# New planning constants for a fused attention and GEGLU kernel

## The chip, the cores and the metric

The kernel runs on one core of one Trainium2 chip. The metric is the device time of one execution in microseconds; the core has a matrix engine (TensorE, PE), a vector engine (VectorE, DVE), a scalar engine (ScalarE, ACT), GpSimd (POOL) and a sync engine (SyncE, SP) that issues the DMAs. Each engine runs its own instructions strictly in the order of the program and waits on semaphores for the others.

## The reference

One transformer block on 2048 rows of width 640: attention with 32 heads of 20 columns behind a LayerNorm, then a gated MLP of width 1728 behind a second LayerNorm, each with its residual.

```python
def _A_ref(x, wqkv, wo):
    B, S, D = x.shape
    H = 32
    Dh = D // H
    qkv = (x @ wqkv).reshape(B, S, 3, H, Dh) ...
    scores = jnp.einsum("bhqd,bhkd->bhqk", q, k) * (Dh ** -0.5)
    p = _softmax(scores, axis=-1)
    o = jnp.einsum("bhqk,bhkd->bhqd", p, v)
    return o ... @ wo

def _B_ref(x, w_gate, w_up, w_down):
    g = jnp.einsum("bsd,df->bsf", x, w_gate)
    u = jnp.einsum("bsd,df->bsf", x, w_up)
    h = _gelu(g) * u
    return jnp.einsum("bsf,fd->bsd", h, w_down)

h = x + _A_ref(_layernorm(x, axis=-1), A_wqkv, A_wo)
h2 = h + _B_ref(_layernorm(h, axis=-1), B_w_gate, B_w_up, B_w_down)
return h2
```

## The kernel before

**Tiles, slots and units.** The queries are worked in eight chunks (SIZES: 512, five of 256, two of 128 rows). The heads form eight groups of four. A *slot* is 512 columns of queries: one head group for the chunk of 512, two for 256, four for 128; there are 32 slots, 0 to 31. Each slot has 64 score tiles of 128 keys by 512 query columns, four of them (one for each head of the group) making a *quad*. The scores of a tile are one row-tiled product, since a head has only 20 columns and four heads sit in four strips of 32 rows (`qk_mms`, L1059). Tiles go through in *units* (`unit`, L1035): alternately three tiles in the PSUM banks 0 to 2 and two in the banks 3 and 4. ACT takes the exponential of a whole unit in one instruction, 1536 or 1024 columns wide (emitted through a helper, so the profile names L437), and writes it to a ring of 19 tiles (`pts`, and a part of `rege`).

**Tiles on DVE.** D_SLOT says how many quads of a slot do not go to ACT but to DVE. Such a tile's scores go to a spare bank (5 or 7), or, for as many of the slot's tiles as D_RING allows, to the third bank of a three-bank unit, which then has only two tiles for ACT. DVE first turns the scores into 16-bit integers (`d_exp`, L972) and, when a quad has its four tiles, makes four terms from them (2048 wide each, L437), whose sum as bf16 stands for the exponential. Each term is a value product of its own. SUMS says how many pairs of terms DVE adds beforehand, each of which saves one value product. D_SPAN spreads the tiles over the slot.

**Value products.** A quad's four tiles meet the values in column tiling: four strips of 32 columns, one for each head, in bank 6 (`pv_op`, L995). `unit` issues them when PV_QUADS quads are complete, two here. Values of a later slot wait until the last product of the slot before is in, and its `epilogue` (L1128) has copied bank 6 to `osb`. The epilogue then normalizes, for most slots through DRAM (`spread`, L1106), for the last ones of a chunk through PE transposes (L1159 to L1203).

**Around it.** Ahead of the first scores stand the first LayerNorm, the transposes of its result (L662), the key, query and value projections (L745, L887), and a bound on the scores (L772, L871, L875) that is subtracted through an extra row of the product. Later projections, and for each finished chunk the output projection (L740), second LayerNorm, transposes (L662 on PE for the chunks in XP_PE, a DMA for the others), gate and up products (L1314 and L740), GELU and down product (L1383 and L740) are filled in between the scores and value products of the next chunk (`post`, L1230). For the last chunk they stand at the end, behind the last exponential.

**What sets the order.** No order is written by hand. Every operation is recorded with an estimated duration and a priority, and a planner in the program (`Sched.schedule`, L100) makes each engine's order when the program is built. It keeps the constants below:

- QK_LEAD, by slot: how long before ACT is due PE is kept free for the next scores (L254).
- PE_AGE, by slot: how long an operation in another tiling may wait before PE changes its tiling for it (L177); the tilings are row, column and full.
- SD_AGE and SD_ROW, by slot: how long a DVE tile's scores wait for a row-tiled stretch (L165).
- P_..., the priorities (a lower number goes first); P_EV those of DVE operations that free a bank, P_KP those of the first key projection, P_RS those of the LayerNorm's statistics, P_ADD those of the residual sums.
- HOLD, K1_AFTER, V_HOLD, Q1_HOLD: evacuations or products of the front that are held back until the bound of the first head group is ready; V_ACT, XN_DVE and K1_ACT: which evacuations of the front go to ACT and which to DVE.
- PAD_MIN: where PE's recent use is low, value products get up to four idle matmuls with a zero operand as filler.

The check that decides how many quads are issued at once:

```python
if n < PV_QUADS and left:
    return
quads = [pv_wait[4 * k:4 * k + 4] for k in range(min(n, PV_QUADS if left or s_ < len(slots) - 1 else 1))]
```

## Time and profile before

| | |
|---|---|
| Median of 3 runs | 867.11 us (866.93 to 867.78) |
| The profiled execution | 867.46 us |
| Its span, first to last instruction | 865.7 us |
| Granted TensorE clock | 1.00 throughout |
| First exponential starts | 33.0 us |
| Exponentials of 1024 columns | 454 |
| Exponentials of 1536 columns | 264 |
| DVE tiles (L972) | 348 |

The span can be read in three parts. In the front the input comes in, is normalized and projected. The middle is the long run of exponentials. At the end the last chunk's MLP runs. A group's mean duration covers the whole of an instruction, while the next one of the same engine already begins, so the distance from start to start is shorter than the mean. The engines' shares are averages over all three parts; the prediction reads them by stretch.

### The profile page before, as it was taken

What the parts mean: (1) busy time and instruction counts of PE and PEld (TensorE: products, weight loads), DVE (VectorE), ACT (ScalarE), POOL (GpSimd) and SP (SyncE); (2) the same over time, 40 slices, a digit from 0 to 9 for tenths busy, and PEclk for the clock granted to TensorE, in tenths of its full rate; (3) what the DMA queues carried; (4) which work ended last, traced back from release to release, by engine and by line L of the source; (5) the groups of instructions that cost most, each with busy time, mean ns of one, the idle gap of its engine ahead of it and who ended that gap; (6) DMA issues with size and microseconds to landing.
All of it is one profiled execution on the core that took longest, in us unless ns stands there. A gap on an engine that the chain in (4) does not pass through costs nothing.

```text
span 865.7 us, 35516 instructions
## 1 busy us (share of the span) xinstructions
PE 835.9 (97%) x16187; PEld 420.8 (49%) x16219; DVE 748.5 (86%) x1371; ACT 839.4 (97%) x806; POOL 93.7 (11%) x268
## 2 busy tenths in 40 slices
PE   7999999999999899999999999999999999999998
PEld 5533332322344344445455555555554556666667
DVE  8859999999898899797899989999999897998344
ACT  7899999999999999999999999999999999999992
POOL 5001111110001210101002010011102110010000
DMA  7211122123102442001110201010101201020000
GB/s 274 84 50 57 32 71 61 46 71 93 53 4 67 128 146 80 16 18 36 53 42 16 36 8 61 5 35 17 49 19 24 58 8 31 19 48 11 2 18 17
DMA packets 47485, 42.54 MB, mean 49 GB/s; under 512 B 18628, under 2 KB 41952, under 8 KB 47336
## 3 DMA queue, kind: packets, MB, share of 16 engines
q1 hardware_dynamic: 47336, 40.27, 16.0%
q8 instruction: 127, 2.08, 1.0%
q14 instruction: 22, 0.18, 0.1%
HBM read 27.95 MB, written 10.26 MB: 44 GB/s over the span
## 4 chain that ended last, share of the span: by engine, by line
ACT 45%; PE 42%; DVE 11%; issue 1%; DVEq 0%
ACT pts L437 30%; ACT rege L437 14%; PE ps L1059 13%; PE ps L437 11%; PE ps L740 10%; PE ps L745 3%; DVE qt_all L437 2%; PE ps L887 2%; DVE rege L437 2%; DVE rege L972 2%; PE ps L1314 1%; DVE qt_all L972 1%; DVE stats L437 1%; ACT qt_all L437 1%; PE ps L1383 1%
## 5 line engine op out<-in xcount | busy, mean ns | idle before, releaser
L437 ACT ACTIVATE pts<-ps 128x1024 bf16<-128x1024 f32 (+1 forms) x496 | 558.3, 1232 | 2.9 <-PE ps L1059 2.1
L1059 PE MATMUL ps<-qt_all,kt_all 32*128 32x256 bf16 (+2 forms) x4096 | 307.1, 273 | 11.2 <-ACT pts L437 5.2
L437 ACT ACTIVATE rege<-ps 128x1024 bf16<-128x1024 f32 (+1 forms) x222 | 247.6, 1192 | 0.4 <-PE ps L1059 0.2
L1059 PEld LDWEIGHTS ps<-qt_all,kt_all 32*128 32x128 bf16 x4096 | 104.2, 92 | 198.1 <-ACT pts L437 83.0
L972 DVE TENSOR_SCALAR rege<-ps 128x512 int16<-128x512 f32 x220 | 148.2, 683 | 19.4 <-PE ps L1059 18.1
L437 PE MATMUL ps<-rege,v_all 128*21 128x256 bf16 (+2 forms) x2201 | 140.3, 286 | 1.3 <-DVE rege L437 0.5
L437 PE MATMUL ps<-pts,v_all 128*21 128x256 bf16 (+2 forms) x2403 | 124.7, 273 | 1.0 <-DVE osb L437 0.8
L740 PE MATMUL ps<-rege,regw 128*32 128x256 bf16 (+1 forms) x2600 | 120.5, 296 | 1.5 <-DVE rege L972 0.5
L972 DVE TENSOR_SCALAR qt_all<-ps 128x512 int16<-128x512 f32 x128 | 86.5, 682 | 11.9 <-PE ps L1059 11.4
L437 DVE TENSOR_SCALAR rege<-rege 128x2048 int16<-128x2048 int16 x141 | 94.5, 686 | 2.5 <-PE ps L437 1.9
L740 PEld LDWEIGHTS ps<-rege,regw 128*32 128x32 bf16 x2600 | 60.4, 96 | 34.6 <-issue 20.1
L437 PEld LDWEIGHTS ps<-rege,v_all 128*21 128x21 bf16 x2201 | 54.1, 91 | 42.7 <-issue 25.2
L437 PEld LDWEIGHTS ps<-pts,v_all 128*21 128x21 bf16 x2403 | 57.0, 91 | 26.1 <-issue 18.4
L740 PE MATMUL ps<-regw,rege 128*32 128x320 bf16 x1296 | 68.1, 301 | 0.7 <-issue 0.4
L437 DVE TENSOR_SCALAR qt_all<-qt_all 128x2048 int16<-128x2048 int16 (+4 forms) x113 | 65.4, 589 | 2.8 <-ACT qt_all L437 1.1
L437 PE MATMUL ps<-qt_all,v_all 128*21 128x256 bf16 (+1 forms) x1264 | 56.4, 264 | 0.8 <-DVE qt_all L437 0.8
L437 DVE TENSOR_SCALAR qt_all<-rege 128x2048 int16<-128x2048 int16 x80 | 53.8, 684 | 1.5 <-PE ps L437 0.9
L745 PE MATMUL ps<-regw 128*128 128x512 bf16 x176 | 52.5, 383 | 2.0 <-issue 1.1
L437 POOL TENSOR_SCALAR rn<-rc 128x16 int32<-128x16 int32 x22 | 6.7, 305 | 393.3 <-DMA rc<-sums 393.1
L1368 DVE TENSOR_TENSOR rege<-rege,ps 128x512 bf16<-128x512 bf16 (+2 forms) x53 | 35.0, 661 | 13.0 <-PE ps L740 6.6
L1314 PE MATMUL ps<-rege,regw 128*128 128x128 bf16 (+1 forms) x420 | 41.0, 238 | 0.0
L740 PEld LDWEIGHTS ps<-regw,rege 128*32 128x32 bf16 x1296 | 30.3, 96 | 19.3 <-issue 11.8
(139 smaller groups left out, 806.2 us busy)
## 6 DMA issues: line engine op xcount, KB each, us to landing
bsum<-rsums SPq DMA_DIRECT2D x88, 64.0 KB, 2.0
rege<-in_A_x_dram SPq DMA_DIRECT2D x5, 640.0 KB, 5.9
q_rows<-regw SPq DMA_DIRECT2D x20, 128.0 KB, 1.7
out_dram<-rege SPq DMA_DIRECT2D x15, 160.0 KB, 1.8
regw<-in_B_w_gate_dram SPq DMA_DIRECT2D x5, 432.0 KB, 3.3
regw<-in_B_w_up_dram SPq DMA_DIRECT2D x5, 432.0 KB, 3.4
kt_all<-k_rows SPq DMA_DIRECT2D x12, 160.0 KB
qt_all<-q_rows SPq DMA_DIRECT2D x12, 160.0 KB
```

The source lines that it names most:

```text
L437: return lambda eng: getattr(eng, method)(*args, **kwargs)
L740: return [lambda eng, j=j: eng.matmul(out()[32 * j:32 * j + 32], l[:, 32 * j:32 * j + 32], r, start=start, stop=stop, tile_position=(0, 32 ...
L745: fn = col4(lambda: bank(bk, n), l, r, k == 0, k == len(steps) - 1) if col else lambda eng, l=l, r=r, k=k: eng.matmul(bank(bk, n), l, r, s ...
L887: w_readers.append(op("pe", lambda eng, i=i, kt=kt, a=a: eng.matmul(bank(bk)[:, i * w:i * w + w], xnT[:, a, kt * 128:(kt + 1) * 128], wv[: ...
L972: d_ops.append(op("dve", lambda eng: eng.tensor_scalar(v[:, 512 * h:512 * h + 512], bank(b), EXP_MUL, -32000.0, ALU.mult, ALU.max), c_dve( ...
L1059: return lambda eng: eng.matmul(out()[:, kk * nq:(kk + 1) * nq], kt_all[32 * j:32 * j + 32, g, kt * 128:(kt + 1) * 128], qt_all[32 * j:32 ...
L1314: lambda eng, a=a, f=f, fi=fi: eng.matmul(bank(bk)[:, fi * nq:(fi + 1) * nq], w[:, a, F0[f]:F0[f] + 128], hnT[:, a, 128 * tb:128 * tb + nq ...
L1368: hdone.append(op("dve", lambda eng, bu=bu, fv=fv, w=w: eng.tensor_tensor(fv, fv, bank(bu, w), ALU.mult), c_dve(w), p, reads=[ku] + hkeys( ...
L1383: f == NF - 1) if cl else lambda eng, f=f, o=o, bk=bk, w0=w0, w1=w1: eng.matmul(
```

## The change

The change was announced as value products issued one quad of key tiles at a time instead of two in all slots, with the order of the rest planned for it. In the diff PV_QUADS stays 2; what differs are constants that the planner and the tables of slots read. Nothing else of the program is touched, so the functions are the same, and the order that comes out differs on PE, DVE, ACT and SP (POOL's is the same).

```diff
-QK_LEAD = (0.68, 0.72, 0.65, 0.6, 0.65, 0.65,) + (0.72,) * 8 + (0.65,) * 3 + (0.72,) * 6 + (0.68,) * 9
+QK_LEAD = (0.68, 0.6, 0.65, 0.6, 0.65, 0.65, 0.72, 0.5, 0.72, 0.72, 0.68, 0.68, 0.72, 0.72,) + (0.65,) * 3 + (0.72,) * 7 + (0.68, 0.6,) + (0.68,) * 6
 ACT_GAP = .012
-PE_AGE = (2.5, 3.0, 5.0, 5.0, 2.5,) + (1.0,) * 4 + (2.0,) + (5.0,) * 3 + (3.0,) * 8 + (1.5,) * 6 + (3.5, 3.0,) + (1.5,) * 3
-SD_AGE = (0.6, 0.6, 0.3,) + (0.6,) * 6 + (0.8,) + (0.6,) * 3 + (0.5, 0.6, 1.0, 0.3, 0.6, 0.8, 0.6, 1.0, 0.5, 1.0, 1.0, 0.5,) + (0.6,) * 7
-SD_ROW = (0,) * 5 + (1.0,) + (0.6,) * 3 + (1.5, 0.6, 0.6, 1.5,) + (0.6,) * 16 + (1.0, 0.6, 0,)
+PE_AGE = (1.0, 1.5, 5.0, 2.0, 2.0,) + (3.5,) * 8 + (3.0,) * 8 + (1.0,) * 11
+SD_AGE = (0.6, 0.6, 0.3,) + (0.6,) * 6 + (0.8,) + (0.6,) * 3 + (0.5, 0.6, 0.6, 0.3, 0.3, 0.6, 0.8, 1.0, 0.5, 1.0, 1.0, 0.5, 0.6, 0.3,) + (0.6,) * 4 + (0.3,)
+SD_ROW = (0, 0.3,) + (0,) * 3 + (1.0,) + (0.6,) * 3 + (1.5, 0.6, 0.6, 1.5, 0.6, 0.6, 0.3,) + (0.6,) * 4 + (0.3,) * 4 + (0.6,) * 5 + (1.0, 0.6, 0,)
...
 PV_QUADS = 2
 PR, PR2 = 13, 6
-D_SLOT = (1,) + (3,) * 26 + (2, 3, 3, 0, 0,)
-SUMS = (0,) + (1,) * 5 + (2, 0, 0, 1, 0,) + (1,) * 3 + (0, 1, 1, 2, 3, 1, 0, 1, 1, 0, 2, 2, 1, 0, 1, 0, 3, 0,)
+D_SLOT = (1,) + (3,) * 18 + (4, 3, 3, 2,) + (3,) * 4 + (2, 3, 3, 0, 0,)
+SUMS = (0,) + (1,) * 5 + (2, 0, 0, 1, 0, 1, 0, 1, 0, 1, 1, 2, 3, 1, 0, 1, 1, 0, 2, 2, 1, 0, 1, 0, 4, 1,)
...
-D_RING = (9,) * 8 + (6,) * 20 + (12,) + (3,) * 3
+D_RING = (9, 9, 6,) + (9,) * 6 + (3, 3,) + (6,) * 17 + (12, 3, 9, 9,)
...
-D_SPAN = (16,) + (18,) * 13 + (17,) + (18,) * 4 + (19,) * 4 + (18,) * 7 + (17, 17,)
+D_SPAN = (16,) + (18,) * 13 + (17,) + (18,) * 4 + (19, 16, 16, 19,) + (18,) * 9
...
-P_EV = 1.5
+P_EV = 1.2
...
-V_ACT = (0, 3)
-XN_DVE = (8, 10, 13, 15)
+V_ACT = (0,)
+XN_DVE = (8, 10, 12, 13, 15)
...
-XP_PE = (0, 6)
-HOLD = 1
-P_KP = 1.6
-K1_AFTER = 2
+XP_PE = (0, 3, 6)
+HOLD = 0
+P_KP = 1.45
+K1_AFTER = 0
 Q1_HOLD = 1
-V_HOLD = 6
+V_HOLD = 2
...
-K1_ACT = ()
+K1_ACT = (0,)
...
-P_RS = 1.45
+P_RS = 1.0
...
-P_ADD = 0.6
+P_ADD = 1.8
```

Counted over the built programs: ACT has 298 + 144 exponentials of 1024 columns (pts + rege; 300 + 154 before) and 201 + 71 of 1536 (196 + 68). DVE has 348 such tiles in both, one pre-sum less, and three copies more. PE has 16230 matmuls for 16219: ten transposes and eight value matmuls more, seven fillers less. SP has two DMA transposes less. The 16 DVE tiles of slot 19 and the 8 of slot 22 were 12 each before.

## The prediction

> **What bounds the kernel now.** I read the profile from the coarse to the fine: busy shares, then busy time by stretch, then who ScalarE (ACT) waited for, then the chain of work in order of time. The busy shares first (engine, busy us, share, instructions):

> ```profile
> PE 835.9 (97%) x16187; PEld 420.8 (49%) x16219; DVE 748.5 (86%) x1371; ACT 839.4 (97%) x806; POOL 93.7 (11%) x268
> ```

> Two engines stand at 97%, so an average settles nothing. The stretches (from:to, length, then busy us of PE, PEld, DVE, ACT, POOL, the granted clock, DMA share, GB/s) separate them:

> ```profile
> 0.00:50.00 50.00, 44.43 (x377) 26.45 (x381) 37.70 (x100) 42.61 (x63) 11.71 (x31) 1.00 0.50 171
> ...
> 500.00:600.00 100.00, 98.37 (x2474) 54.96 (x2472) 96.02 (x174) 99.92 (x95) 10.18 (x32) 1.00 0.10 27
> 600.00:700.00 100.00, 99.05 (x2355) 52.58 (x2352) 96.13 (x172) 99.80 (x94) 12.73 (x32) 1.00 0.13 33
> ...
> 840.00:866.00 26.00, 23.23 (x326) 19.66 (x322) 13.26 (x35) 9.49 (x16) 0.00 (x0) 1.00 0.05 15
> ```

> ACT is full from 50 to 840 us and empty only at both ends; VectorE (DVE) is nearly full from 500 to 700. ACT's waits for scores (us in total, times, longest) are tiny:

> ```profile
> ACT pts L437 <- PE ps L1059: 2.1, 6, 0.6
> ...
> ACT rege L437 <- PE ps L1059: 0.2, 1, 0.2
> ```

> But busy spans of neighbours overlap, so small lateness hides in them. I took it from starts instead. In the timeline a 1536-wide exponential starts the next one after 1.33 us, a 1024-wide one after 0.904 at best; 454 of 1024 and 264 of 1536 (groups by shape: 300 + 154 and 196 + 68) are 410.4 + 351.1 = 761.5 us. Summing what each of the 718 lies above its best gives 18.2 us of lateness, nearly all in some 130 exponentials that are about 0.1 us late each. That, the first exponential's start (33.0 us) and what follows the last one (841.6 to 865.7, 24.1 us) is all that a new order can win; what it can lose has no such limit.

> TensorE (PE) is the second wall. The chain, where it runs through PE (start, us, engine, line, count):

> ```profile
> 505.00 0.55 PE ps L740 x20
> 505.55 0.33 PE ps L1059 x6
> 505.87 0.55 PE ps L437 x16
> ...
> 510.56 0.49 DVE rege L1388
> 511.05 0.61 DVE rege L1351
> ```

> Prices from it: 16 value matmuls of 256 columns (four column strips at once) take 0.55, which is 16 / 4 x 256 / 2.4 GHz = 0.43 and about 0.11 for the change between row, column and full tiling; a score group takes 0.33, 0.21 and the same 0.11. Over all changes of tiling between 34 and 839 us the shortest cost is 0.104 to 0.108 and the median 0.113. A DVE operation on 512 PSUM columns or 2048 int16 costs 0.60 to 0.61 in a row.

> **The change part by part.** Only constants change, PV_QUADS stays 2, and the built program shows value matmuls in the same runs as before (of 8, 16 and 24 in a row: 195, 126, 34 before; 181, 118, 35 after). So I price it as another order of nearly the same work.

> *Work.* ACT loses 12 exponentials of 1024 and gains 8 of 1536 (1700 tiles in both): -12 x 0.904 + 8 x 1.330 = -0.2 us. PE gets 11 more matmuls: 10 transposes (chunk 3 now transposed on PE instead of by 2 DMAs), 8 more value matmuls because there is one pre-sum less, 7 filler matmuls less; its row strips also collide more often; with 3 more changes of tiling (1572 for 1569), the sum up to the last score group is 767.8 us for 763.6. It costs nothing by its amount, since 806 us pass there. DVE: one 1.22 us pre-sum less, three 0.48 copies more, about even. SP's queue issues two transposes less and swaps neighbours; no score waited for a DMA in the profile of before (ACT's waits name PE alone), so I take nothing for it. [...]

> *Front, to the first exponential.* Up to 20 us the orders are the same. From the first common pair of transpose groups to the first scores PE issues 28 instead of 29 matmuls of 512 columns (0.216 each), 30 instead of 28 of 160 (0.07) and the same 60 transposes: -0.1 us; PE has no gap there to speak of, so this holds. Behind the last key chunk, before had a 0.6 us evacuation (L783, at 31.07) ahead of L875, which L1059's first scores need, and L875 started at 31.67 though L871 had finished at about 31.4. After, that evacuation is ACT's and L875 is first: -0.25. The cover that could go is the ACT table load (1.28, done at 32.36 before), which now stands behind one more 0.58 evacuation; it bounds the loss at +0.5, and the 0.64 that ACT waited before the first exponential bounds the gain at -1.0 with the rest. I take -0.4.

> *Middle.* Slots 0 to 8 (to about 250 us) have the same DVE order and nearly the same PE order. Then the DVE share per slot (D_SLOT) gets uneven: slot 19 has 16 DVE tiles instead of 12, slot 22 only 8. I cut both programs' orders into slots and priced them with the rows above. For slot 19 ACT has 20.6 us of exponentials and its other work (23.8 before) and PE 21.8 (23.5); for slot 20 ACT 25.6 and PE 25.8 (24.7 and 23.7). DVE has, from the first tile of slot 16 to that of slot 22, 8.2 us more than before, 5.2 of them in slot 20 (28.8 us, in a slot that lasted 25.4). Before, those six slots (426.9 to 577.7) lasted 150.8 us with 142.8 of DVE busy.

> To see where this reaches ACT I went from one score group to the next: a group may start when PE has done what stands ahead of it and the exponential two before has freed its banks (0.08); the exponential follows 0.25 after 0.21 of scores; ACT falls behind by what PE is late. Held against before, this rule finds 3.1 us of the 18.2, at most 0.39 at one place: it sees only lateness from too much PE work between two groups. For after it finds 8.7, in lumps: 0.6 in slot 16, 1.5 in slot 19, and 2.9 at one place, the seventh unit of slot 20; the rest is in pieces under 0.4. There, between two neighbouring score groups, stand 28 + 104 column matmuls of 256 columns with one DVE tile's scores between: (28 + 104) / 4 x 0.1067 = 3.52, two score groups 0.43, four changes 0.45, together 4.4 us, against exponentials of 1.33 + 0.904 = 2.23 to cover them; with the 0.08, 0.21 and 0.25, ACT stands still for 2.7 to 2.9 us. Nothing gives that back, because ACT has no slack later. The middle: 8.7 - 3.1 = +5.6 us. Bounds: -1 (the 15.1 us of fine lateness shrink by more than the lumps add) and +9 (DVE's 8.2 us reach ACT in full, beside 0.8 at slot 16).

> *End.* The same 22.3 us of PE work follow the last score group. Before, the last value products came after 33 of the 70 up-projection matmuls of 128 columns, and PE stood some 0.7 us in the stretch to L1252 at 846.07 and 0.2 inside L1252 (10 matmuls in 1.53 us for 1.33). After, they come after 27, so the osb copy, L1159, L1169 and L681 start 0.7 us earlier, and L1252 is interleaved with L1383. Gain at most 0.9, loss at most 0.5 (an L1388 of 0.48 now stands ahead of the last LayerNorm's scaling, and 6 instead of 10 L1383 cover the L690 copy behind it). I take -0.4.

> *Sum.* -0.2 - 0.4 + 5.6 - 0.4 = +4.6 us on the profiled span of 865.7: 870.3. That execution took 867.46, and the median of the runs shown is 867.11, 1.4 over the span, so I forecast 871.7.

> **The rivals.**

> *About the same (867).* The stretch at slot 20 is there, but the fine lateness falls: twelve 1024-wide exponentials less, on which nearly all lateness lies (449 x 0.035 = 15.7 us), is only 0.4 us by proportion, so this needs a fifth to a third of the 15.1 us to go. For it: from slot 9 on the order differs throughout, and lateness of 0.1 us is below what my rule sees. Against: nothing in the order shows a gain.

> *Faster (865).* Front -1.0, end -0.9, exponentials -0.2, and the lumps largely covered. It decides from the point where DVE's backlog is drained before slot 20's seventh unit. Against it: PE executes in order, and 4.4 us of its work stand between two score groups whatever DVE does.

> *DVE becomes the bound (875).* PE's order at slot 20 waits on DVE terms too: value products of slot 19 need them, and the scores in banks 2, 5 and 7 need DVE to free them. Before, 8.0 us of DVE idle lay in these six slots; if none can be used, the 8.2 us come through whole: 867.1 + 8.2 + 0.8 - 1.0 = 875.1. For it: DVE was busy all of 554.8 to 577.7.

> *The change does what its words say.* 425 quads in ACT's tiles, issued singly, would make up to 212 more pairs of changes of tiling, 0.226 each, +48 us: 915. The run lengths above exclude it but for a mistake of mine.

> **How the numbers follow.** About 0.2% (1.7 us) is what a measurement of this kernel tells from no change. Chances: my forecast with lumps of 2 us or more, 0.53; DVE as the bound, 0.19; about the same, 0.16; faster, 0.11; the words, 0.01. So slower 0.73, same 0.16, faster 0.11. The likeliest case's own range is 869 to 874. The range that should hold 8 in 10 starts at 866.3 (most of "same") and ends at 876.5 (DVE's full backlog and 1.4 more for waits that are not in a PE sum).

> **What would show it.** Right: ACT's idle time or stretched starts grow by some 5 us, with a single gap of 2 to 4 us in slot 20 (about 530 to 545 us) released by PE's scores, no such gap before 250 us, a first exponential near 32.6 us, and 23.7 us after the last one. Wrong: no gap over 1 us in slots 19 and 20; a gap released by DVE tiles over several slots (then DVE is the bound); a later first exponential; or value matmuls in runs of half the length.

## The result, and the profile after

The kernel after takes 874.41 us (median of 4 runs, 873.21 to 876.41), the kernel before 867.29 on the same chip (4 runs, 866.93 to 867.78): a ratio of 1.0082, interval 1.0070 to 1.0094. It is 0.8% slower, 7.1 us; the forecast was 871.7, the range 866.3 to 876.5. The profiled execution took 874.65, its span 872.8, which is 7.1 over the span before too.

The busy shares of the page (engine, busy us, share, instructions):

```profile
PE 839.9 (96%) x16198; PEld 423.1 (48%) x16230; DVE 746.5 (86%) x1373; ACT 840.1 (96%) x801; POOL 100.1 (11%) x268
```

ACT's work hardly grew (840.1 us for 839.4), so the 7 us are time in which ACT stood still or started late. The stretches of the kernel after (length, then busy us of PE, PEld, DVE, ACT, POOL, clock, DMA share, GB/s) show where:

```profile
0.00:50.00 50.00, 43.64 (x374) 27.23 (x377) 37.58 (x101) 41.71 (x62) 11.70 (x31) 0.97 0.50 171
500.00:600.00 100.00, 97.76 (x2357) 53.27 (x2361) 92.52 (x170) 95.05 (x89) 10.18 (x32) 1.00 0.07 21
600.00:700.00 100.00, 98.58 (x2300) 51.06 (x2298) 92.28 (x165) 99.64 (x94) 13.31 (x32) 1.00 0.14 34
850.00:873.00 23.00, 20.21 (x256) 16.93 (x253) 10.48 (x30) 6.52 (x13) 0.00 (x0) 1.00 0.05 16
```

Two rows differ from before. Between 500 and 600 us ACT is busy 95.05 of 100 where it was 99.92. And in the first 50 us the granted clock is 0.97 where it was 1.00. ACT's waits (us in total, times, longest) name what the first row hides:

```profile
ACT pts L437 <- PE ps L437: 3.3, 1, 3.3
...
ACT pts L437 <- PE ps L1059: 2.3, 5, 0.9
...
ACT rege L437 <- PE ps L437: 1.3, 1, 1.3
```

Two waits are new, of 3.3 us (slot 20) and 1.3 us (slot 16), and both are for value products (L437), not for scores (L1059). The longer one stands in ACT's timeline (start, us, engine, line, form, count, idle before and its releaser):

```profile
530.34 2.37 ACT L437 ACTIVATE rege<-ps 128x1024 bf16<-128x1024 f32 x2
532.58 1.05 ACT L437 ACTIVATE pts<-ps 128x1024 bf16<-128x1024 f32 x1
536.96 3.71 ACT L437 ACTIVATE pts<-ps 128x1536 bf16<-128x1536 f32 x3 [3.33 <-PE ps L437]
```

PE's timeline over the same stretch:

```profile
532.97 0.45 PE L1059 MATMUL ps<-qt_all,kt_all 32*128 32x256 bf16 x8
533.35 0.59 PE L740 MATMUL ps<-regw,rege 128*32 128x320 bf16 x12
533.87 0.39 PE L1059 MATMUL ps<-qt_all,kt_all 32*128 32x256 bf16 x4
...
535.63 0.62 PE L740 MATMUL ps<-rege,regw 128*32 128x256 bf16 x16
536.08 0.39 PE L437 MATMUL ps<-qt_all,v_all 128*21 128x256 bf16 x8
536.29 0.61 PE L437 MATMUL ps<-pts,v_all 128*21 128x256 bf16 x16
536.73 1.50 PE L740 MATMUL ps<-rege,regw 128*32 128x256 bf16 x48
...
538.70 0.39 PE L1059 MATMUL ps<-qt_all,kt_all 32*128 32x256 bf16 x6
```

The scores of the waiting exponential are done by 533.4 and those of the next by 534.3. But ACT writes into a ring of 19 tiles; places come free when the value products on ring tiles (`pts`) at 536.29 have run, and the exponential starts at their end (536.90; it starts at 536.96). The trace shows no wait of PE for DVE between 520 and 540 us. The next score group, at 538.70, is the other end of the block that the prediction priced. Without the ring ACT would have met it: from 532.58 on, exponentials of 0.904, 1.330 and 0.904 end at 535.72, and those scores end at 539.09, 3.4 us later. The two stops lie in one hole, and PE is busy 3.37 of the 3.40 us from 533.6 to 537.

Slot 16's wait is of the same kind: the scores of that exponential are done by 433.22, it starts at 434.53, and the value products on ring tiles in front of it run from 433.86 to 434.47. The two stops of slot 19 (0.84 and 1.00 us) are released by scores.

I summed again, from starts, what each exponential lies above its best. The first nine slots agree with before within 0.03 us each.

| | before | after |
|---|---|---|
| first exponential starts | 33.00 | 33.41 |
| lateness, all slots | 18.3 | 25.0 |
| of it slot 16 (largest) | 0.7 (0.2) | 1.8 (1.4) |
| slot 19 | 0.6 (0.2) | 2.3 (1.0) |
| slot 20 | 0.5 (0.2) | 3.6 (3.5) |
| from the last exponential's end to the end | 24.1 | 24.3 |

So +0.4 in front, +6.7 of lateness, -0.2 for the exponentials' own length and +0.2 at the end: 7.1.

### The profile page after: what moved, and what is told of

It reads as the page before. It is cut to its first block, busy times and chain, and to the rows that moved or that the text cites. A ratio compares the mean times of both kernels' runs of the same rounds, so it can differ in the third digit from the quotient of the medians.

```text
span 872.8 us, 35521 instructions
## 1 busy us (share of the span) xinstructions
PE 839.9 (96%) x16198; PEld 423.1 (48%) x16230; DVE 746.5 (86%) x1373; ACT 840.1 (96%) x801; POOL 100.1 (11%) x268
## 4 chain that ended last, share of the span: by engine, by line
PE 47%; ACT 30%; DVE 21%; issue 1%; POOL 0%; DVEq 0%
ACT pts L437 21%; PE ps L1059 14%; PE ps L437 11%; PE ps L740 11%; ACT rege L437 9%; DVE qt_all L437 6%; DVE rege L972 3%; PE ps L745 3%; PE ps L1314 3%; DVE rege L437 3%; DVE qt_all L972 3%; PE ps L887 2%; DVE rege L1368 1%; DVE stats L437 1%; PE ps L1383 1%
## 5 line engine op out<-in xcount | busy, mean ns | idle before, releaser
L437 ACT ACTIVATE pts<-ps 128x1024 bf16<-128x1024 f32 (+1 forms) x499 | 563.7, 1231 | 6.7 <-PE ps L437 3.3
L1059 PE MATMUL ps<-qt_all,kt_all 32*128 32x256 bf16 (+2 forms) x4096 | 309.3, 272 | 12.4 <-ACT pts L437 7.1
L437 ACT ACTIVATE rege<-ps 128x1024 bf16<-128x1024 f32 (+1 forms) x215 | 242.4, 1198 | 1.4 <-PE ps L437 1.3
L1059 PEld LDWEIGHTS ps<-qt_all,kt_all 32*128 32x128 bf16 x4096 | 105.7, 92 | 199.4 <-ACT pts L437 75.8
L972 DVE TENSOR_SCALAR rege<-ps 128x512 int16<-128x512 f32 x220 | 147.9, 683 | 24.2 <-PE ps L1059 23.0
L437 PE MATMUL ps<-rege,v_all 128*21 128x256 bf16 (+2 forms) x2163 | 136.8, 287 | 1.9 <-DVE rege L437 0.9
L437 PE MATMUL ps<-pts,v_all 128*21 128x256 bf16 (+2 forms) x2433 | 122.6, 272 | 0.4 <-issue 0.2
L740 PE MATMUL ps<-rege,regw 128*32 128x256 bf16 (+1 forms) x2600 | 119.6, 296 | 2.7 <-DVE rege L972 0.6
L437 DVE TENSOR_SCALAR rege<-rege 128x2048 int16<-128x2048 int16 x141 | 94.5, 686 | 2.4 <-PE ps L437 1.9
L740 PEld LDWEIGHTS ps<-rege,regw 128*32 128x32 bf16 x2600 | 60.2, 96 | 37.3 <-issue 21.1
L437 PEld LDWEIGHTS ps<-rege,v_all 128*21 128x21 bf16 x2163 | 53.3, 91 | 41.9 <-issue 23.0
L437 PEld LDWEIGHTS ps<-pts,v_all 128*21 128x21 bf16 x2433 | 56.2, 91 | 26.1 <-issue 19.2
L437 DVE TENSOR_SCALAR qt_all<-qt_all 128x2048 int16<-128x2048 int16 (+4 forms) x113 | 65.4, 587 | 3.0 <-ACT qt_all L437 1.9
L740 PE MATMUL ps<-regw,rege 128*32 128x320 bf16 x1296 | 64.4, 301 | 0.3 <-DVE rege L1368 0.2
L437 PE MATMUL ps<-qt_all,v_all 128*21 128x256 bf16 (+1 forms) x1280 | 57.1, 264 | 1.1 <-DVE qt_all L437 1.0
L437 DVE TENSOR_SCALAR qt_all<-rege 128x2048 int16<-128x2048 int16 x80 | 54.4, 686 | 0.8
L437 POOL TENSOR_SCALAR rn<-rc 128x16 int32<-128x16 int32 x22 | 6.0, 271 | 389.2 <-DMA rc<-sums 389.0
L1368 DVE TENSOR_TENSOR rege<-rege,ps 128x512 bf16<-128x512 bf16 (+2 forms) x53 | 35.0, 661 | 13.2 <-PE ps L740 5.9
L1314 PE MATMUL ps<-rege,regw 128*128 128x128 bf16 (+1 forms) x420 | 39.2, 238 | 0.6 <-DVE rege L1368 0.5
L740 PEld LDWEIGHTS ps<-regw,rege 128*32 128x32 bf16 x1296 | 29.4, 96 | 18.0 <-issue 9.8
```

Source lines behind the costliest of these rows:

```text
L437: return lambda eng: getattr(eng, method)(*args, **kwargs)
L740: return [lambda eng, j=j: eng.matmul(out()[32 * j:32 * j + 32], l[:, 32 * j:32 * j + 32], r, start=start, stop=stop, tile_position=(0, 32 ...
L972: d_ops.append(op("dve", lambda eng: eng.tensor_scalar(v[:, 512 * h:512 * h + 512], bank(b), EXP_MUL, -32000.0, ALU.mult, ALU.max), c_dve( ...
L1059: return lambda eng: eng.matmul(out()[:, kk * nq:(kk + 1) * nq], kt_all[32 * j:32 * j + 32, g, kt * 128:(kt + 1) * 128], qt_all[32 * j:32 ...
L1314: lambda eng, a=a, f=f, fi=fi: eng.matmul(bank(bk)[:, fi * nq:(fi + 1) * nq], w[:, a, F0[f]:F0[f] + 128], hnT[:, a, 128 * tb:128 * tb + nq ...
L1368: hdone.append(op("dve", lambda eng, bu=bu, fv=fv, w=w: eng.tensor_tensor(fv, fv, bank(bu, w), ALU.mult), c_dve(w), p, reads=[ku] + hkeys( ...
```

## The experiments

The first four ask what makes the lumps of slots 19 and 20; the kernel before took 867.03 us on that chip (7 runs).

**The even D_SLOT put back into the kernel after.**

```diff
-D_SLOT = (1,) + (3,) * 18 + (4, 3, 3, 2,) + (3,) * 4 + (2, 3, 3, 0, 0,)
+D_SLOT = (1,) + (3,) * 26 + (2, 3, 3, 0, 0,)
```

> The changed kernel with D_SLOT alone set back to three quads in every slot from 1 to 26. Theory of the late terms: the lumps of slots 19 and 20 go (no exponential over 1 us late there, 2.3 + 3.6 us of lateness become about 1.0), slot 16 keeps its single stop of 1.4 us, and the time falls by 4 to 5.5 us, from 874.4 to 869 to 870.5. Rival, that the loss comes from the other constants (D_RING, the tables of ages, the front): the time stays above 872.5. Rival, that DVE's load as a whole is the bound: the load of all slots together is the same, so lateness spreads but less than half of it goes.

Measured: 873.88 us, ratio 1.0076 (1.0061 to 1.0091). The lumps of slots 19 and 20 are gone (0.9 and 0.4 in all), slot 16's stays at 1.43, and lateness falls by 3.5 to 21.6, as expected. The time doesn't follow: from the start of the last exponential to the end it takes 28.9 us, where before takes 25.2 and after 25.4. I had assumed that the end stays what it is. It does not: the planner lays out the whole program anew, and this order leaves 2.2 us more PE work behind the last score group (25.8 us busy for 23.6).

**The uneven D_SLOT alone, in the kernel before** (the same two lines, exchanged).

> The kernel before with D_SLOT alone taken from the change (4 quads in slot 19, 2 in slot 22). Theory of the late terms: a stop or two in slot 20, 1.5 to 2.5 us together, and 868.5 to 870.5 us: less than in the changed kernel, because there the constants around it make it worse. Rival, that the uneven share costs nothing by itself: within 0.8 us of before.

Measured: 877.01 us, ratio 1.0114 (1.0099 to 1.0129), 6.5 us over the range expected. Slot 20 is late by 2.9 (2.2 in one stop), all lateness 3.6 over before: D_SLOT makes this lump in either kernel. Again the end costs more, 30.9 us for 25.2. The front costs 1.2 more, but not through D_SLOT: up to slot 19 the order of PE is that of before, and in this execution the granted clock from 12 to 22 us was 0.83 (more on this in the last section).

**The one pre-sum of slot 19 taken out of the kernel after** (SUMS, entry 19: 1 becomes 0), so that PE multiplies two DVE tiles instead of their sum and DVE has one operation of 1.22 us less.

> The changed kernel with SUMS of slot 19 at 0 instead of 1: one pre-sum of 1.2 us less on DVE near the end of slot 19, one value product more. Theory of the late terms: the stop of 3.5 us in slot 20 shrinks by more than the 1.2 us of DVE work taken out, to 0.5 to 1.8 us, slot 19 keeps its stops, and the time falls by 1.5 to 3 us to 871.4 to 873. Rival, DVE's load: at most 1.2 us go, and the stop stays over 2.2 us.

Measured: 884.88 us, ratio 1.0206 (1.0189 to 1.0223). The stop in slot 20 shrinks to 1.6 as expected, and slot 19 keeps its 2.3. The time misses what was expected by some 12 us: the end takes 36.7 us, 11.3 more than in the kernel after.

**Eight pre-sums in slot 19** (SUMS, entry 19: 1 becomes 8).

> The changed kernel with SUMS of slot 19 at 8 instead of 1: seven more pre-sums on DVE (8.5 us) and seven value products less, so PE has 1.5 us less work. Theory of the late terms: the last value product of slot 19 comes up to 8 us later, the ring of 19 tiles is full in the first third of slot 20, and ACT stops there once for 7 to 10 us, beside some 5 us in slot 19; 883 to 888 us. Rival, that PE's work between score groups is the cause: less PE work, 873 or less. Rival, that DVE's load alone counts: lateness spread over slots 19 to 23 without a single stop over 4 us.

Measured: 895.7 us (2 runs), ratio 1.033 (1.0307 to 1.0352). One stop of 13.2 us in slot 20, where 7 to 10 were expected, two of 2.9 and 3.3 in slot 19, and the end 31.4 us; the time is 8 us over what was expected. ACT, then PE, then the stretch (length, PE, PEld, DVE, ACT, POOL):

```profile
539.31 1.07 ACT L437 ACTIVATE pts<-ps 128x1024 bf16<-128x1024 f32 x1
553.46 3.71 ACT L437 ACTIVATE pts<-ps 128x1536 bf16<-128x1536 f32 x3 [13.07 <-PE ps L437]
```

```profile
540.76 1.05 PE L437 MATMUL ps<-kt_all,zer 128*32 128x512 bf16 x16
...
552.57 0.40 PE L437 MATMUL ps<-qt_all,v_all 128*21 128x256 bf16 x8 [1.17 <-DVE qt_all L437]
552.79 0.61 PE L437 MATMUL ps<-pts,v_all 128*21 128x256 bf16 x16
```

```profile
539.50:553.50 14.00, 11.44 (x310) 7.30 (x314) 14.00 (x22) 0.93 (x2) 0.00 (x0) 1.00 0.06 18
```

Here the chain is in the open. DVE is busy all of 14.00 us, PE fills the hole with products of zeros (`zer`) and background work, then waits 1.17 us for DVE's last term; the value products on ring tiles follow, and ACT runs again. The stop goes 1.6, 3.5, 13.2 with 0, 1 and 8 pre-sums: the later DVE's last terms of slot 19, the longer it is. Whether DVE itself holds PE in the kernel after, or the order that was planned with DVE in mind, these runs don't tell; the last test does.

**What the announcement says, done.** PV_QUADS becomes 1, first in the kernel before, then in the kernel after. For the four kernels of this test and the next, the kernel before took 867.87 us (14 runs).

```diff
-PV_QUADS = 2
+PV_QUADS = 1
```

> The kernel before with value products issued one quad at a time (PV_QUADS 2 to 1), which is what the change's announcement says and the change doesn't do. The new order has 1600 changes of tiling for 1569 and 3.9 us more of PE work behind the last score group (25.5 for 21.55). Theory (late lumps in the middle, and an end that is as long as the PE work left for it, at the 1.5 to 1.8 us per us that the first four experiments showed): lateness +4.9 us, nearly all in slot 4 as one stop of about 3.6 us, 31 changes at 0.113 = 3.5 us that are covered, end +6 to +7; time 876 to 880. Rival A (the prediction's price of the words, 212 pairs of changes): +48 us, 915. Rival B (only the middle counts, the ends of the first four experiments were accidents): 871 to 873. Rival C (quads are nearly always joined in the order anyway): 866.5 to 868.

Measured: 879.41 us, ratio 1.0129 (1.0112 to 1.0145). Lateness +6.7 (one stop of 3.4 early, 1.4 and 0.9 late), the end 30.9 us.

> The kernel after with the same constant set to 1. 1614 changes of tiling for 1572, 9.2 us more of PE work behind the last score group (30.8 for 21.55). Theory: lateness +4.8 us over the kernel after, with a stop of some 6 us in slot 4 and one of 3 in slot 18, none over 1.5 in slot 20; end +14 to +16 us; time 892 to 896. Rival A (prediction's price of the words): 920. Rival B (only the middle counts): 878 to 880.

Measured: 887.65 us, ratio 1.0226 (1.0212 to 1.0241). Stops of 6.4, 3.7 and 1.6 us, the end 35.3 us. The kernels get 11.5 and (against the bridged kernel after, below, on the same chip) 13.1 us slower, the first as the theory with its two terms has it, the second 4 us under it (its end grew by 9.9 us, not by 14 to 16), and both far from the +48 of the prediction's rival: the planner still puts quads side by side, so there are 31 and 42 changes of tiling more, not 424. The largest stops came within 0.7 us of those read off the built order beforehand (3.6; 6 and 3); the 1.6 in slot 20 was not foreseen.

**PE kept busy ahead of the first transposes.** 14 more filler matmuls of 256 columns, at a price of one in the plan, so that the rest of the order stays.

```diff
-op("pe", lambda eng, wb=wb: eng.matmul(...),
+op("pe", [lambda eng, wb=wb: eng.matmul(...)] * (15 if i == 46 else 1),
```

> The kernel before with 14 more of the 256-column filler matmuls ahead of the first transposes and nothing else changed in the order, so that PE doesn't stand idle for 2.1 us there. Theory (in the kernel after PE's half rate in the first transposes, 0.71 for 0.45 us, comes from a 3.2 us idle stretch; before escapes it narrowly in its profiled execution): first exponential at 33.0 as before or up to 0.3 later, the five transposes of L662 at 0.45, mean granted clock no lower than before's, time 866.3 to 867.5. Rival (the clock takes no notice of the idle stretch): the same time. Rival 2 (the fillers delay the transposes): first exponential up to 2 us later, 867.5 to 869.

Measured: 866.39 us (11 runs), ratio 0.9982 (0.9973 to 0.9991): faster than before by 0.2%.

> The kernel after with the same 14 fillers. Theory: the five transposes of L662 take 0.45 us instead of 0.71, no slice of the front shows a granted clock under 0.95, the first exponential starts at 32.5 to 33.0 instead of 33.4, and the time is 0.4 to 1.2 us under the kernel after: 873.2 to 874.0 on a chip where that has 874.4; lumps in the middle unchanged (1.4, 2.0, 3.5 us in slots 16, 19, 20). Rival (the late front of the kernel after belongs to its order, not to the clock): first exponential at 33.3 or later, time 874.2 to 875. Rival 2 (half rate is a matter of chance at every start): L662 at 0.71 again.

Measured: 874.56 us (5 runs), ratio 1.0076 (1.0062 to 1.0089). PE in the kernels before, after and after with the bridge:

```profile
2.92 7.97 PE L607 MATMUL ps<-zer,ident 128*128 128x256 bf16 x47 [2.92 <-POOL ident L437]
12.95 0.45 PE L662 MATMUL ps<-ident,rege 128*128 128x128 bf16 x5 [2.06 <-DVE rege L437]
```

```profile
2.91 6.83 PE L607 MATMUL ps<-zer,ident 128*128 128x256 bf16 x47 [2.91 <-POOL ident L437]
12.95 0.71 PE L662 MATMUL ps<-ident,rege 128*128 128x128 bf16 x5 [3.20 <-DVE rege L437]
```

```profile
2.92 9.76 PE L607 MATMUL ps<-zer,ident 128*128 128x256 bf16 x61 [2.92 <-POOL ident L437]
12.95 0.45 PE L662 MATMUL ps<-ident,rege 128*128 128x128 bf16 x5 [0.27 <-DVE rege L437]
```

Five transposes take 0.71 after 3.20 us of idle PE, 0.45 after 2.06 or 0.27. With the bridge the kernel after has its first exponential at 32.81, not 33.41. The time misses the 873.2 to 874.0 that were expected. In the profiled execution, the longest of the five, PE stood 0.76 us at 753 us with nothing to wait for that the trace shows, and slot 28 was late by 1.1 in one stop; why the median doesn't show the 0.6 us either is open.

**The front's new constants alone**, eight of them (V_ACT, XN_DVE, HOLD, P_KP, K1_AFTER, V_HOLD, K1_ACT, P_RS), in the bridged kernel before. The edit also sets Q1_HOLD to 0, which the change leaves at 1; with these constants the program built with Q1_HOLD = 1 has the same instructions in the same order on every engine. For this and the next two tests the kernel before took 867.76 us (21 runs).

```diff
-V_ACT = (0, 3)
+V_ACT = (0,)
...
-K1_ACT = ()
+K1_ACT = (0,)
...
```

> The kernel before with the 14 bridging fillers and the eight front constants of after (V_ACT, XN_DVE, HOLD, P_KP, K1_AFTER, V_HOLD, K1_ACT, P_RS); middle and end keep before's order. Theory (the prediction's front step of -0.4 us was right in sign, and the later front of the kernel after was the clock alone): first exponential at 32.6 to 32.9 instead of 33.0, time 0 to 0.4 us under the bridged kernel before. Rival (the front's new order is what makes the kernel after start later): first exponential at 33.3 or later, time 0.3 to 0.8 us over.

Measured: 866.00 us (11 runs), ratio 0.9985 (0.9976 to 0.9993), the lowest median here. The first exponential starts at 32.81, with 33.01 in the bridged kernel before, and the end stays what it was: 25.3 us from the last exponential's start.

**D_RING alone**, in the bridged kernel before.

```diff
-D_RING = (9,) * 8 + (6,) * 20 + (12,) + (3,) * 3
+D_RING = (9, 9, 6,) + (9,) * 6 + (3, 3,) + (6,) * 17 + (12, 3, 9, 9,)
```

> The kernel before with the 14 bridging fillers and one planning constant of after, D_RING. Theory (D_RING, not D_SLOT, is what puts the lump into slot 16, since it stayed when D_SLOT alone was undone): a single stop of about 1.4 us in slot 16, none over 0.7 in slots 19 and 20, lateness of slots 15 to 22 1.0 to 1.4 us above the bridged kernel before. Its order leaves 2.6 us more PE work behind the last score group (24.2 for 21.55), so the stretch from the last exponential's start to the end grows by 3 to 4 us (25.3 to 28.5 or 29.5), and slot 28 may be late by 1 more; time 5 to 7 us over the bridged kernel before. Rival A (only the middle counts): 1 to 3 us over. Rival B (slot 16's lump comes from other constants): no stop over 0.7 there.

Measured: 876.58 us, ratio 1.0096 (1.0082 to 1.0110). The stop in slot 16 is there, 1.43 us as in the kernel after, and slots 19 and 20 have none. The time is 10 us over the bridged kernel, where 5 to 7 were expected: slots 28 to 30 are late by 3.3 more in all, and the end takes 31.4 us, where at most 29.5 were expected.

**A longer end by a known amount**, in the bridged kernel before: each of two matmuls issued ten times.

```diff
-op("pe", lambda eng, ...: eng.matmul(bank(bk, 320), ident[:], hs, start=True, stop=False),
+op("pe", [lambda eng, ...: eng.matmul(bank(bk, 320), ident[:], hs, start=True, stop=True)] * 9 +
+         [lambda eng, ...: eng.matmul(bank(bk, 320), ident[:], hs, start=True, stop=False)],
```

> The kernel before with the 14 bridging fillers, and each of the two matmuls of L1249, which run about 2 us after the last score group, issued ten times instead of once: 18 x 0.133 = 2.4 us of PE work more behind the last score group, in an order otherwise the same. Theory A (PE is full to the end, so work left for the end costs its own length): span and time 2.2 to 2.6 us over the bridged kernel before; then the 1.5 to 2.8 us per us that re-planned kernels showed are the left work plus a worse order of the end. Theory B (the end has slack on PE, and what re-planned kernels lose there is waiting for DVE and ACT): under 1 us. Theory C (a delay at this place grows on the way, as value products, LayerNorm and the down projection follow each other): 3.5 us or more.

Measured: 868.75 us (10 runs), ratio 1.0009 (1.0000 to 1.0019), 2.4 over the bridged kernel's 866.39 (with before at 867.76 and 867.87), and 2.5 in the span: work left for the end costs its own length, theory A. The stretches from the last exponential's start to the end, in the kernel before, in this one, and with D_RING (length, then PE busy first):

```profile
840.50:865.70 25.20, 22.73 (x318) 19.20 (x314) 12.76 (x35) 8.99 (x16) 0.00 (x0) 1.00 0.04 14
```

```profile
839.40:866.90 27.50, 24.99 (x336) 20.95 (x333) 12.92 (x35) 9.02 (x16) 0.00 (x0) 1.00 0.04 13
```

```profile
843.30:874.70 31.40, 26.52 (x356) 21.71 (x357) 16.61 (x43) 12.43 (x19) 0.00 (x0) 1.00 0.04 12
```

Before and with the two matmuls repeated PE has 2.5 us of idle time there (25.20 - 22.73 and 27.50 - 24.99). With D_RING it has 3.8 us more work and 4.9 us of idle time, the largest piece a wait of 1.1 us for DVE. This dear end is work left over plus new waits.

**DVE made faster under an unchanged order**, to settle what sets the stop in slot 20. The kernel after, bridged; the 16 term operations of slot 19 work on a quarter of their columns, so a part of that slot's weights is left at old values.

```diff
-I("tensor_scalar", a, v, 0.25, off, ALU.mult, ALU.add)
+I("tensor_scalar", *(x[:, 0:512 if tile[0] == 19 else 2048] for x in (a, v)), 0.25, off, ALU.mult, ALU.add)
```

> The kernel after with the 14 bridging fillers; the 16 term operations that DVE runs for slot 19 (tensor_scalar on 128x2048 int16, 0.60 us each) work on the first 512 of their columns only, so a part of slot 19's weights is left at old values. The order on PE and ACT is the same to the last instruction; DVE gets some 5 to 7 us of slack there. Theory A (as the prediction put it: PE runs in order, and its block between two score groups sets the stop whatever DVE does): the stop in slot 20 stays at 3.0 to 3.5 us, time within 0.5 us of the bridged kernel after (874.6 beside 867.9). Theory B (DVE's late last terms hold the value products at run time, and PE's block only fills the hole): the stop falls under 1.5 us, slot 19's two stops of 0.8 and 1.0 fall too, time 2 to 4 us less. Between them (part PE's order, part DVE): a stop of 1.5 to 3.0.

Measured: 874.22 us, ratio 1.0071 (1.0054 to 1.0088); before took 868.90 on this chip. First the stretch in the bridged kernel after, then in this one, then the stop:

```profile
500.00:545.00 45.00, 43.89 (x1049) 24.13 (x1050) 41.88 (x72) 40.05 (x38) 2.50 (x10) 1.00 0.11 33
```

```profile
500.00:545.00 45.00, 43.97 (x1060) 24.45 (x1056) 36.81 (x74) 40.30 (x38) 2.15 (x10) 1.00 0.12 33
```

```profile
536.64 4.62 ACT L437 ACTIVATE pts<-ps 128x1536 bf16<-128x1536 f32 x4 [3.09 <-PE ps L437]
```

DVE is busy 5.1 us less (36.81 for 41.88) and ACT gains 0.25: the stop goes from 3.48 to 3.24, slot 19's two stops of 0.84 and 1.00 stay to the hundredth. Theory A holds: at run time it is PE's order that keeps ACT standing. With the pre-sum tests I read it so: DVE acts through the plan, which puts background work ahead of value products whose operands it expects late. That last step, inside the planner, no run shows by itself.

## Why the prediction was right, point by point

- *Exponentials, -0.2.* By count and row it holds; nothing in the runs speaks against it.
- *Front, -0.4; measured +0.4.* The order gains 0.2 (32.81 for 33.01, both bridged). The 0.64 that ACT waited before the first exponential did go, but the cover I named went too: the evacuation at L780 now stands ahead of the table load, which has become the last thing that the first exponential waits for (it ends at 33.37, the exponential starts at 33.41). The other 0.6 (33.41 for 32.81) is the half clock after the idle stretch, and it is no part of the change: the kernel before has the same stretch, and 30 of its 49 runs listed in these tests show a mean clock under 1.000, though not the profiled one. The prediction had no term for it. The rival of a later order is excluded.
- *Middle, +5.6; measured +6.7.* Right in place, a little small. Lumps of 0.6, 1.5 and 2.9 were forecast for slots 16, 19 and 20; their lateness rose by 1.1, 1.7 and 3.1. No gap came before 250 us, as said. The 2.4 by which its prices divide columns shows in the trace of before: 7 matmuls of 512 columns took 1.51 us and 140 of 128 took 7.82, 0.216 and 0.056 each, so 384 columns are 0.160 us, 2.4 per ns. The rule undersized slot 16 most: one stop of 1.43, which the full ring sets and of which the rule sees only PE's scores. Its cause is D_RING (the same 1.43 from D_RING alone), that of slots 19 and 20 D_SLOT.
- *Who releases the stop.* The prediction said PE's scores; the trace says PE's value products, because the ring of 19 tiles fills before the scores run short. The rule knew no ring. It found the stop because the block of PE work it priced lies in the same hole. That the scores would have ended it within 0.1 us of where the ring did is luck for the size. What held for a reason is that PE's order sets it: with the terms shortened the stop stayed, as "whatever DVE does" had it.
- *DVE as the bound (875).* The measured 874.41 lies nearer to it than to the forecast, but its mechanism is excluded as put: 5.1 us less of DVE's work in that stretch gave 0.25 back. What is true of it is that DVE's planned lateness shapes PE's order (0, 1 and 8 pre-sums).
- *End, -0.4; measured +0.2.* The earlier value products gain nothing: from the last exponential's start on PE is busy 22.8 of 25.4 us where it was 22.7 of 25.2, so its idle time, which was to shrink, is 2.6 us for 2.5.
- *Sum.* +4.6 forecast, +7.1 measured: front 0.8 short, middle 1.1, end 0.6. With the clock at full in both fronts the gap is no smaller: bridged, the medians differ by 874.56 - 866.39 = 8.2 us, so there the sum is 3.6 short.
- *The words.* Rightly set aside, but priced four times too high (+48 for 11.5): the rival counted pairs of tiling changes where the planner makes few of them.

Not settled: why the bridged kernel before gains some 0.7 us even over those runs of before with full clock (866.39 for 867.07, the median of three). In its profile slots 28 and 29 are late by 1.1 us where before's had 2.6, and before's PE stood 0.39 us in slot 28 with nothing to wait for in the trace; no run here separates the two.

## What to carry to other kernels

In a program that a planner lays out, walk the built order from one score group to the next and price what stands between them, with the buffers that must come free: the stops found so came within about 1 us of the measured ones, but for the 13.2 us where 7 to 10 were expected. Then count what is left behind the last one as well: the 2.4 us of work left there by the repeated matmuls cost 2.4 us, and in seven of the eight kernels that were planned again the end grew by 3 to 11 us, at least as much as any of them gained in the middle. The eighth, with the front's constants, kept its end. So a single constant put back need not undo its part of a change, because everything after it may be planned anew; only edits that left the order behind them alone (the bridge, the front's constants, the repeated matmuls, the shortened terms) measured one thing.

## What the hardware showed unexpectedly

PE also stood still now and then with nothing in the trace to wait for, in an order that was the same in another execution without it. The row of the bridged kernel after:

```profile
754.11 0.34 PE L1059 MATMUL ps<-qt_all,kt_all 32*128 32x128 bf16 x6 [0.76 <-issue]
```

ACT lost 1.1 us to it. With the shortened terms PE has the same order and doesn't stop there. What causes it is open. Smaller pauses of this kind stand in other traces, 13 in that of the kernel after, 2.4 us together and 0.3 at most; they may be no more than missing records, since that trace holds 16198 of 16230 matmuls.
